# An attention and GEGLU block: the GEGLU part in a written order on every engine, gate logits on ScalarE, first loads in two slices, and every second turn of the attention with one block product more

## The chip, the core and the metric

The kernel runs on one core of a Trainium2 chip. The time is the device time of one execution in microseconds (us). A profile is one execution recorded by the hardware: it shows each engine's instructions (PE is TensorE's matmuls, PEld its weight loads, DVE VectorE, ACT ScalarE, POOL GpSimd, SP the queue of SyncE that issues most transfers). "L60" is line 60 of the kernel; all matmuls go through one helper at that line, so they are told apart by their tiles.

## What is computed

```
a = attention(x, w_qkv, w_o)            # 16 heads of 28, 2048 positions, width 448, no mask
g = x @ w_gate; u = x @ w_up            # 448 -> 1792
b = (gelu_tanh(g) * u) @ w_down         # 1792 -> 448
s = sigmoid(x @ gate_w)                 # one number per position
out = s * a + (1 - s) * b
```

All arrays are fp32, batch 1. The kernel keeps nearly fp32 precision by cutting an operand into a rounded part `hi` (format fp32r, a ScalarE copy) and the remainder `lo` (a subtraction on VectorE or GpSimd); a product of two such operands is hi x hi + hi x lo + lo x hi.

## The kernel before, in words

**Blocks of products.** A block is a result of 128 x 512. Its 448 long contraction is cut into 7 slices of 64 rows, so with the three products of the split a block has 21 matmuls (`UNITS`). A matmul uses 64 rows of the array, half of it; two blocks on the two row halves (g = 0, 1) advance side by side.

**Stage 1** loads and splits x and the weights, and makes Q and K (`pq`, 14 pairs of blocks), which are stored to DRAM, then V and the gate logits (`v_pair`, the logits copied by VectorE at L200). A bound on the scores is computed; VectorE, TensorE and ScalarE then pass a branch (`rows`, L295) around a slow path that this data does not need, with a hint put after the sixth `v_pair`. Loads go through raw buffers of one slice each (`AHEAD` of them).

**Stage 2, the attention.** For each head, key tile and half of the queries (a *turn*), `scores` makes a PSUM tile `sc` of 1024 columns by four matmuls of 64 rows, and ScalarE takes its exponential into `pt`. Since scores use one row half at a time, the other half takes up to four (`RATE`) products of the up and gate projections into the tile `pu` (one PSUM buffer): 68 (`NOUT`) of the 112 blocks of both projections are made here. A finished block is copied by VectorE to `u` (L429) and stored to DRAM (`ud`). After each four key tiles, at the third turn (`LATE`) of the next four, `values` adds these four tiles' `pt` times V into `po`. A *period* is these eight turns. After a head's last, `finish` copies `po` to `o` on VectorE, sends the sums through DRAM (`dend`, `r`), takes the reciprocal, sends it back in another layout (`rdend`, `rb`), multiplies, and stores the head to `od`. Two blocks run in an `sc` tile ahead of the first score (`two_blocks`), and what is left of the blocks at the end.

**Stage 3, the FFN.** The 14 tiles of the hidden dimension (f) go in seven chunks of two, in the order of `ORDER`. For each f and each half b the gate blocks `pg` that are still missing are made on TensorE, the others are loaded (`gs`); gelu (ACT), times `u` (DVE), split (ACT, DVE) give `hl2`. Then 16 tiles of `pd` (128 x 448, six matmuls each, four PSUM buffers) are added into `acc` on VectorE with the gate (`down`). For chunks 2 and 3 `project` puts attention output times WO in between (11 matmuls a tile); O is loaded through one raw buffer `oraw` and split on ACT, POOL and DVE (`load_o`, L591 to L603). The weights of an f come as `hraw` to `half` (one raw buffer, `load_half`) and as `draw` to `w` (`load_f`). In the last chunk the result goes to a tile named `gs` (two buffers) and is stored from there.

**What sets the order.** Instructions handed to `pin` (tc.keep_in_program_order) stay in the order of the program among themselves; the others are placed by a scheduler that works with its own costs. Before, all matmuls are pinned, and the loads and splits of stage 1; `finish`, the `u` copies and nearly all of stage 3 on DVE, ACT and SP are not. Each engine then executes its list in order and waits at an instruction whose inputs are not there.

## Time and profile before

| | |
|---|---|
| median of 3 runs | 1083.91 us (1083.66 to 1086.1) |
| the profiled execution | 1081.29 us, span of its trace 1079.5 us |
| granted TensorE clock, whole span | 0.99 |
| TensorE busy | 1047.9 us, 97% of the span |
| start to the last V product | 0 to 113.1 us |
| first products of the attention stage to the last `po` | 119.2 to 776.15 us |
| FFN, to TensorE's end | 776.15 to 1072.75 us |
| tail | 6.75 us |

A row of a timeline is: start, length, engine, line, operation, output <- inputs, count, and in brackets the idle time of the engine ahead of it with what ended it. A row of the chain of waits is: start, length, what was waited for or worked at.

### The profile page before, as it was taken

The numbers are of one execution on the slowest core, as the hardware profiler recorded it, in microseconds if no ns is written. First come the engines' busy times: TensorE is split into PE (matmuls) and PEld (weight loads), VectorE is DVE, ScalarE is ACT, GpSimd is POOL, SyncE is SP. The second block draws the span as 40 slices with busy tenths as digits, with TensorE's granted clock in tenths as the row PEclk, the third lists the DMA queues.
The fourth block names the chain that finished last, engine by engine and source line by source line (L and its number), as shares of the span: only waits on it lengthen the run. The fifth ranks groups of instructions, "written<-read, shape, count | busy, mean of one in ns | idle before, by whom it ended". The sixth has DMA issues, their size and how long they took to land.

```text
span 1079.5 us, 20134 instructions
## 1 busy us (share of the span) xinstructions
PE 1047.9 (97%) x8257; PEld 733.0 (68%) x8257; DVE 332.9 (31%) x515; ACT 612.3 (57%) x740; POOL 69.2 (6%) x47
## 2 busy tenths in 40 slices
PE   8999799999999999999999999999888999999997
PEld 6889555655665665565566556556576889888886
DVE  4552112111111111111111111111287656646644
ACT  5332377777777877777787777778344304131320
POOL 3524200000000000000000000000001011100000
PEclk9999899999999999999999999999998999999999
DMA  6795544345345344344354444422476314122313
GB/s 188 250 380 148 133 115 134 106 124 138 103 128 144 89 134 137 102 126 132 101 141 118 111 135 114 123 81 67 152 208 199 103 57 120 49 59 80 105 49 137
DMA packets 68321, 138.19 MB, mean 128 GB/s; under 512 B 15744, under 2 KB 25984, under 8 KB 62784
## 3 DMA queue, kind: packets, MB, share of 16 engines
q1 hardware_dynamic: 67904, 136.33, 42.8%
q8 instruction: 66, 1.08, 0.4%
q10 hardware_dynamic: 320, 0.52, 0.2%
q14 instruction: 31, 0.25, 0.1%
HBM read 96.44 MB, written 40.37 MB: 127 GB/s over the span
## 4 chain that ended last, share of the span: by engine, by line
PE 77%; DMA 4%; ACT 3%; DVE 3%; issue 2%; SPq 0%; DVEq 0%; ACTq 0%
PE po L60 21%; PE sc L60 21%; PE pu L60 16%; PE pd L60 11%; PE pg L60 8%; ACT pt L378 2%; DMA out<-gs 1%; DMA u<-ud 1%; DVE ohl L601 1%; DMA oraw<-in_wo 1%; DVE gs L578 1%; DMA oraw<-od 1%; DMA draw<-in_wd 1%; DVE g L554 0%; DMA gs<-ud 0%
## 5 line engine op out<-in xcount | busy, mean ns | idle before, releaser
L378 ACT ACTIVATE pt<-sc 128x1024 f32<-128x1024 f32 x512 | 477.7, 1041 | 170.6 <-PE sc L60 169.5
L60 PE MATMUL sc<-Q,K 64*128 64x512 f32 x2048 | 413.8, 399 | 0.6 <-ACT pt L378 0.4
L60 PEld LDWEIGHTS sc<-Q,K 64*128 64x128 f32 x2048 | 314.5, 184 | 83.3 <-issue 50.3
L60 PE MATMUL pu<-X,half 64*128 64x512 f32 x1344 | 317.4, 387 | 0.0
L60 PEld LDWEIGHTS pu<-X,half 64*128 64x128 f32 x1344 | 247.1, 184 | 33.9 <-issue 1.7
L60 PE MATMUL po<-pt,V 128*32 128x512 f32 x2048 | 234.4, 598 | 0.0
L60 PE MATMUL pd<-w,hl 128*128 128x448 f32 x672 | 145.5, 373 | 9.8 <-DVE acc L575 5.0
L60 PEld LDWEIGHTS po<-pt,V 128*32 128x32 f32 x2048 | 60.2, 110 | 139.5 <-issue 135.8
L429 DVE COPY u<-pu 128x512 f32<-128x512 f32 x64 | 43.8, 685 | 348.9 <-PE pu L60 289.4
L60 PEld LDWEIGHTS pd<-w,hl 128*128 128x128 f32 x672 | 126.4, 190 | 28.1 <-DVE acc L575 6.2
L60 PE MATMUL pg<-X,half 64*128 64x512 f32 x924 | 106.9, 388 | 0.0
L60 PEld LDWEIGHTS pg<-X,half 64*128 64x128 f32 x924 | 88.1, 184 | 18.5 <-issue 2.7
L60 PE MATMUL pq<-X,WQK 64*128 64x512 f32 x588 | 69.2, 394 | 3.1 <-ACT X L161 2.5
L60 PEld LDWEIGHTS pq<-X,WQK 64*128 64x128 f32 x588 | 56.1, 188 | 16.4 <-ACT X L161 3.3
L527 ACT ACTIVATE w<-draw 128x448 fp32r<-128x448 f32 x14 | 8.1, 578 | 92.8 <-PE pd L60 70.2
L575 DVE SCALAR_TENSOR_TENSOR acc<-pd,gate,acc 128x448 f32<-128x448 f32 x80 | 52.8, 681 | 17.0 <-PE pd L60 16.9
L599 POOL CAST ohl<-oraw 64x512 fp32r<-64x512 f32 x4 | 2.4, 606 | 800.2 <-DMA oraw<-od 698.9
L555 ACT ACTIVATE hl<-g 128x512 fp32r<-128x512 f32 x56 | 33.9, 629 | 24.8 <-DVE g L554 20.6
L554 DVE TENSOR_TENSOR g<-g,u 128x512 f32<-128x512 f32 x56 | 36.7, 687 | 33.3 <-ACT g L553 28.5
L556 DVE TENSOR_TENSOR hl<-g,hl 128x512 fp32r<-128x512 f32 x56 | 36.7, 689 | 9.2 <-ACT hl L555 8.3
L553 ACT ACTIVATE g<-pg 128x512 f32<-128x512 f32 x44 | 24.1, 593 | 26.3 <-PE pg L60 26.3
L60 PE MATMUL pd<-WO,ohl 128*128 128x448 f32 x176 | 36.7, 367 | 0.0
(65 smaller groups left out, 449.2 us busy)
## 6 DMA issues: line engine op xcount, KB each, us to landing
Q<-qkd SPq DMA_DIRECT2D x128, 224.0 KB
ud<-u SPq DMA_DIRECT2D x68, 256.0 KB
qkd<-hl SPq DMA_DIRECT2D x28, 512.0 KB
K<-qkd SPq DMA_DIRECT2D x64, 224.0 KB
u<-ud SPq DMA_DIRECT2D x56, 256.0 KB
rb<-rdend SPq DMA_DIRECT2D x64, 64.0 KB
hraw<-in_wu SPq DMA_DIRECT2D x28, 128.0 KB
od<-o SPq DMA_DIRECT2D x64, 56.0 KB
```

What stands on the lines that cost most here:

```text
L60: return pin(nc.tensor.matmul(o, lhsT, rhs, start=start, stop=stop))
L378: nc.scalar.activation(pt, sc, AF.Exp, scale=SCALE)
L429: nc.vector.tensor_copy(u, block["p"])
L527: nc.scalar.activation(hi, draw, AF.Copy)
L553: nc.scalar.activation(g, pg, AF.Gelu_apprx_tanh)
L554: nc.vector.tensor_tensor(g, g, u, OP.mult)
L555: nc.scalar.activation(hl[:, 0], g, AF.Copy)
L556: nc.vector.tensor_tensor(hl[:, 1], g, hl[:, 0].bitcast(F32), OP.subtract)
L575: nc.vector.scalar_tensor_tensor(acc[:, t], p, g1, acc[:, t], OP.mult, OP.add)
L578: nc.vector.scalar_tensor_tensor(y, p, g1, acc[:, t], OP.mult, OP.add)
L599: nc.gpsimd.tensor_copy(O[0:64, 3], o[0:64, 3])
L601: nc.vector.tensor_tensor(O[64:, 3], o[64:, 3], O[64:, 3].bitcast(F32), OP.subtract)
```

## The change

- **Stage 1.** Raw buffers hold two slices (5 of 1024 columns in place of 8 of 512); the first pieces go on two queues (SP and ACT's); a tiny ACT operation stands ahead of the first split; splits have another order, the later lo parts all on GpSimd. The gate logits are copied by ScalarE, and the branch hint is given for TensorE and ScalarE only.
- **Stage 2.** No blocks ahead of the first score. 66 blocks in place of 68 are made here (64 in `pu`, 2 with the `rest` at the end, in an `sc` tile, all in one `run`), so two gate blocks more are left for the FFN. In the turn ahead of `values` products are given only to finish a block, and if the number of products since the last `values` is odd, one product more is issued right ahead of `values`. `free` is aligned at `values`.
- **Stage 3.** Everything is pinned: loads, splits, gelu, accumulations and stores stand on every engine in the order of the program. The list `side_work` holds operations of which `step` issues one after the matmuls of each `down` or `project` tile, ahead of its accumulation: the rest of the gelu work, the four parts of the WO and O splits (now ScalarE and VectorE, no GpSimd), and `prepare` of the two f's of the next chunk. The result is written over `acc` and stored from there.

```diff
-NOUT = 68
+NOUT = 66
 ORDER = (0, 4, 1, 5, 2, 6, 3, 7, 8, 9, 10, 11, 12, 13)
-AHEAD = 8
-HL = 13
+AHEAD = 5
+HL = 12
 PAD = 112
-WARM = 9
+WARM = 12
...
-                d = pin(nc.vector.tensor_copy(gate[:, 0, i:i + 1], p[g][:, D:D + 1]))
-            return m, a, d
-
+                a = pin(nc.scalar.activation(gate[:, 0, i:i + 1], p[g][:, D:D + 1], AF.Copy))
+            return m, a
...
+        load(slice(0, 1))
+        for (c, srcs), a in ((pieces("x00")[0], 1), (pieces("w0")[1], 0)):
+            for g in range(2):
+                pin(nc.scalar.dma_start(out=raws[a][side(g), c], in_=srcs[g]))
+        issued = 2
+        while issued < AHEAD:
+            load()
+        pin(nc.scalar.activation(zero[:, 0:1], zero[:, 0:1], AF.Copy))
+        first = [parts(a, raws[i]) for i, a in enumerate(SPLITS[-1])]
+        for i, b in ((0, 0), (1, 0), (1, 1), (2, 0), (2, 1), (0, 1), (3, 0), (3, 1), (4, 0)):
+            r, hi, lo = first[i][b]
+            pin(nc.scalar.activation(hi, r, AF.Copy))
+            pin(nc.vector.tensor_tensor(lo, r, hi.bitcast(F32), OP.subtract))
+        done = len(first)
...
         def values(h, kt):
+            free[:] = [max(free)] * 2
             if kt == 0:
...
         def unit():
 
-            nonlocal hold
+            nonlocal hold, beside
             product(block)
+            beside += 1
             if block["n"] == len(UNITS):
+                put(block)
                 hold = 3
...
-        two_blocks()
...
-                    spaced(h, kt, half, 0 if due and count == LATE or count == LATE + 1 and h + kt > 3 else RATE)
-                    if due and count == LATE:
+
+                    turn = due and count == LATE
+                    if turn or count == LATE + 1 and (h or kt > 3):
+                        n = 0
+                    elif due and count == LATE - 1:
+                        n = 0 if block["n"] in (0, len(UNITS)) else RATE
+                    else:
+                        n = RATE + (h == 0 and kt <= ENDS[0] + 1)
+                    spaced(h, kt, half, n)
+                    if turn:
+
+                        hold = 0
+                        if beside % 2 and left():
+                            run([[unit], []] if block["g"] == 0 else [[], [unit]])
                         for a in due:
                             values(*a)
-                        due, hold = [], 0
+                        due, hold, beside = [], 0, 0
                 ready.append((h, kt))
                 if kt in ENDS:
                     ready, due, count = [], ready, 0
-        hold = 0
-        run([[], [unit] * left()] if block.get("g") else [[unit] * left(), []])
-        while NOUT - 1 - block["at"] >= 2:
-            two_blocks()
+
+        rest = [dict(block)]
+        sc = psc.tile([P, 1024], F32, name="sc")
+        for c in range(2):
+            start(sc[:, c * 512:(c + 1) * 512])
+            rest.append(dict(block))
+        todo = [[], []]
+        for b in rest:
+            todo[b["g"]] += [lambda b=b: product(b)] * (len(UNITS) - b["n"])
+        run(todo)
+        for b in rest:
+            put(b)
         for a in due:
             values(*a)
-        hold = 0
-        while left():
-            unit()
-            hold = 0
+        assert block["at"] == NOUT - 1
...
+        def load_w(f):
             draw = gp.tile([P, TB], F32, name="draw")[:, 0:D]
-            nc.sync.dma_start(out=draw, in_=wd[f * P:(f + 1) * P])
-            hi, lo = w[:, hi:hi + D], w[:, lo:lo + D]
-            nc.scalar.activation(hi, draw, AF.Copy)
-            nc.vector.tensor_tensor(lo, draw, hi.bitcast(F32), OP.subtract)
-            WD[f] = hi, lo
+            w = gp.tile([P, 2, TB], F32R, name="w", bufs=4)[:, :, 0:D]
+            pin(nc.sync.dma_start(out=draw, in_=wd[f * P:(f + 1) * P]))
+            pin(nc.scalar.activation(w[:, 0], draw, AF.Copy))
+            pin(nc.vector.tensor_tensor(w[:, 1], draw, w[:, 0].bitcast(F32), OP.subtract))
+            WD[f] = w
...
+        def tail(f, i, tb, pg):
+            u = tp.tile([P, TB], F32, name="u")
+            pin(nc.sync.dma_start(out=u, in_=ud[0, f, :, tb * TB:(tb + 1) * TB]))
+            if pg is None:
+                pg = tp.tile([P, TB], F32, name="gs", bufs=2)
+                pin(nc.sync.dma_start(out=pg, in_=ud[1, f, :, tb * TB:(tb + 1) * TB]))
+            g = tp.tile([P, TB], F32, name="g")
+            hl = HL2[i, tb]
+
+            def gelu():
+                pin(nc.scalar.activation(g, pg, AF.Gelu_apprx_tanh))
+                pin(nc.vector.tensor_tensor(g, g, u, OP.mult))
+
+            def parts():
+                pin(nc.scalar.activation(hl[:, 0], g, AF.Copy))
+                pin(nc.vector.tensor_tensor(hl[:, 1], g, hl[:, 0].bitcast(F32), OP.subtract))
+
+            return [gelu, parts]
+
+        def tails(f, i, tbs, pgs):
+            a, b = (tail(f, i, tb, pg) for tb, pg in zip(tbs, pgs))
+            return [a[0], b[0], a[1], b[1]]
...
+        def load_wo():
+            raw = wpo.tile([P, 4, TB], F32, name="oraw")[:, :, 0:D]
+            pin(nc.sync.dma_start(out=raw, in_=wo))
+            for b in range(4):
+                yield lambda b=b: (pin(nc.scalar.activation(WO[:, b], raw[:, b], AF.Copy)),
+                                   pin(nc.vector.tensor_tensor(WO[:, 4 + b], raw[:, b], WO[:, b].bitcast(F32), OP.subtract)))
+
...
+        def load_o(tb):
+            s = slice(tb * TB, (tb + 1) * TB)
+            o = wpo.tile([P, 4, TB], F32, name="oraw")
+            pin(nc.sync.dma_start(out=o[:, 0:3], in_=od[0:3 * P, s].rearrange("(b p) n -> p b n", p=P)))
+            pin(nc.sync.dma_start(out=o[:, 3], in_=od[3 * P:, s].unsqueeze(0).to_broadcast([2, 64, TB])))
+            O = OHL[tb] = wpo.tile([P, 7, TB], F32R, name="ohl")
+            for b in range(4):
+                r = slice(64, P) if b == 3 else slice(0, P)
+                lo = 3 if b == 3 else 4 + b
+                yield lambda b=b, r=r, lo=lo: (
+                    pin(nc.scalar.activation(O[:, b], o[:, b], AF.Copy)),
+                    pin(nc.vector.tensor_tensor(O[r, lo], o[r, b], O[r, b].bitcast(F32), OP.subtract)))
+
+        side_work = []
...
+        def step():
+            if side_work:
+                side_work.pop(0)()
+
+        def down(n, tb, chunk):
...
+                step()
                 g1 = gate[:, 2, t:t + 1]
...
+                    pin(nc.vector.scalar_tensor_tensor(acc[:, t], p, g1, acc[:, t], OP.mult, OP.add))
+                    pin(nc.sync.dma_start(out=out[0, t * P:(t + 1) * P], in_=acc[:, t]))
...
+        def prepare(f):
+            if here(f, 1):
+                load_half(1, f, by_act, pin)
+            load_w(f)
+
+        for f in chunks[0]:
+            prepare(f)
+        early = {}
+        for n, chunk in enumerate(chunks):
+            nxt = chunks[n + 1] if n + 1 < len(chunks) else ()
             for b in range(2):
                 for i, f in enumerate(chunk):
-                    if b == 0 and n * FC + i + 1 < NF:
-                        load_f(ORDER[n * FC + i + 1])
-                    for tb, hl in zip((b, b + 2), hidden(f, b)):
-                        hls.setdefault(tb, []).append(hl)
+                    if not here(f, b):
+                        if (n, b) not in early:
+                            for a in tails(f, i, (b, b + 2), (None, None)):
+                                a()
+                    else:
+                        side_work += gate_blocks(f, i, b)
+                        if (b, i) != (1, FC - 1):
+                            while side_work:
+                                step()
             if n == 1:
-                load_wo()
-            for i, tb in enumerate((0, 2, 1, 3)):
-                if n in (1, 2) and i % 2 == 1:
-                    load_o((n - 1) * 2 + i // 2)
-                down(n, tb, hls[tb])
-                if n in (2, 3) and i % 2 == 0:
-                    project((n - 2) * 2 + i // 2)
+                side_work += load_wo()
+            for k, tb in enumerate((0, 2, 1, 3)):
+                if (n, k) == (1, 1):
+                    side_work += load_o(0)
+                down(n, tb, chunk)
+                if n in (2, 3) and k in (0, 3):
+                    while side_work:
+                        step()
+                    at = (n - 2) * 2 + k // 3
+                    project(at)
+                    if at < NTB - 1:
+                        side_work += load_o(at + 1)
+                if nxt and k == 1:
+                    side_work += [lambda f=f: prepare(f) for f in nxt]
+                    for i, f in enumerate(nxt):
+                        if not here(f, 0):
+                            side_work += tails(f, i, (0, 2), (None, None))
+                            early[n + 1, 0] = 1
+            while side_work:
+                step()
```

How the written order reads on the engines, at three places. First TensorE around two successive `values` in the middle of the attention. Before, every period is alike (Q and K carry their buffer's number):

```order
L60 MATMUL pu<-X,half 128x512
L60 MATMUL sc<-Q_1441,K_1442 128x512 x8
L60 MATMUL po<-pt,V 32x512 x16
L60 MATMUL sc<-Q_1441,K_1442 128x512 x4
L60 MATMUL pu<-X,half 128x512
```

Now, the one with the product more:

```order
L60 MATMUL pu<-X,half 128x512
L60 MATMUL sc<-Q_1422,K_1423 128x512 x8
L60 MATMUL pu<-X,half 128x512
L60 MATMUL po<-pt,V 32x512 x16
L60 MATMUL sc<-Q_1422,K_1423 128x512 x5
L60 MATMUL pu<-X,half 128x512
```

A `pu` product of the next block stands between the eight score matmuls and `po`; in the period behind it the block needs one product less, and five score matmuls follow `po` alone.

Second, VectorE from the last head's `o` on, where the FFN begins. Before:

```order
L392 COPY o<-po 128x512
L556 TENSOR_TENSOR hl_10382<-g,hl_10382 128x512
L556 TENSOR_TENSOR hl_10388<-g,hl_10388 128x512
L528 TENSOR_TENSOR w<-draw,w 128x448 x2
L398 RECIPROCAL r<-r 128x16
L554 TENSOR_TENSOR g<-g,u 128x512 x3
```

Now:

```order
L403 COPY o<-po 128x512
L409 RECIPROCAL r<-r 128x16
L415 TENSOR_TENSOR o<-o,rb 128x512
L541 TENSOR_TENSOR w<-draw,w 128x448
L238 TENSOR_TENSOR half<-hraw,half 128x896
L541 TENSOR_TENSOR w<-draw,w 128x448
L558 TENSOR_TENSOR g<-g,u 128x512 x2
```

The reciprocal and the product with `rb` now stand ahead of the FFN's first splits; before, FFN work stood between and around them, and the first `half` ahead of `o`.

Third, VectorE in the downs of a late chunk (the L622 rows are the accumulations), now:

```order
L562 TENSOR_TENSOR hl_13_10293<-g,hl_13_10293 128x512
L622 SCALAR_TENSOR_TENSOR acc<-pd,gate,acc 128x448 x5
L238 TENSOR_TENSOR half<-hraw,half 128x896
L541 TENSOR_TENSOR w<-draw,w 128x448
L622 SCALAR_TENSOR_TENSOR acc<-pd,gate,acc 128x448
L238 TENSOR_TENSOR half<-hraw,half 128x896
L541 TENSOR_TENSOR w<-draw,w 128x448
L622 SCALAR_TENSOR_TENSOR acc<-pd,gate,acc 128x448 x7
```

The lo parts of both weights of both next f's stand around the accumulation of the ninth tile; before, the scheduler had spread them over the chunk.

183 lines of the change are left out of this document (58 added, 125 removed).

## The prediction

> **What bounds the kernel now.** I read the page's busy times and its chain first, then a table by stage, then the timelines of the places that the change touches.
>
> ```profile
> PE 1047.9 (97%) x8257; PEld 733.0 (68%) x8257; DVE 332.9 (31%) x515; ACT 612.3 (57%) x740; POOL 69.2 (6%) x47
> PE 77%; DMA 4%; ACT 3%; DVE 3%; issue 2%; SPq 0%; DVEq 0%; ACTq 0%
> ...
> 119.18:126.43 7.25, 6.41 (x42) 5.27 (x42) 0.69 (x1) 0.00 (x0) 0.00 (x0) 0.80 0.00 1
> 126.43:776.15 649.72, 646.22 (x5484) 388.79 (x5485) 98.12 (x149) 481.93 (x518) 0.00 (x0) 1.00 0.42 120
> 776.15:1072.75 296.60, 286.80 (x1776) 247.52 (x1772) 184.61 (x267) 87.89 (x142) 16.39 (x8) 0.99 0.34 105
> 1072.75:1079.50 6.75, 0.00 (x0) 0.00 (x0) 1.95 (x4) 0.00 (x0) 0.00 (x0) 0.88 0.37 136
> ```
>
> The columns of a stage are its length, then PE, weight loads, DVE, ACT and POOL, the granted clock, the DMA share and GB/s. TensorE is busy 97% of the span and carries 77% of the chain. So only three things can move the time: fewer or better paired matmuls, fewer gaps between them, and the ends where it has nothing. In the attention DVE is busy 98 of 650 us; in the FFN it is 185 of 297. There an engine that must work in a written order has the least slack.
>
> **The entry into the attention.** The rows are TensorE's, then VectorE's, then SyncE's.
>
> ```profile
> 109.66 3.42 PE L60 MATMUL pq<-WV,X 64*128 64x450 f32 x32
> 119.18 6.41 PE L60 MATMUL sc<-X,half 64*128 64x512 f32 x41 [6.11 <-DVEq L295]
> 126.43 0.49 PE L60 MATMUL sc<-X,half 64*128 64x512 f32 x1 [0.84 <-DVE u L429]
> 114.12 0.16 DVE L200 COPY gate<-pq 128x1 f32<-128x1 f32 x1 [0.28 <-ACT V L199]
> 111.10 1.43 SPq L345 DMA_DIRECT2D Q<-shd  x2
> ```
>
> TensorE ends the V products at 113.1 and stands 6.11 us until DVE's sequencer has passed the branch at L295: DVE still has gate logits to copy there, the last at 114.12. Then come the two blocks of `two_blocks` (6.4 us at a clock of 0.80), a stall of 0.84 on their copy, and the first score at about 126.4. Afterwards ScalarE copies the logits, DVE reaches the branch earlier, and both blocks are gone from here. The first score then needs only the Q rows, whose last load is issued by 112.5 and about 1 us later in the new order; with a landing some 2 us on (an estimate) it starts near 115.3: **-11.1**. It cannot start before 113.1 (-13.3); had DVE still to be waited for until 119.2, only 7.2 would go. The blocks' 42 products are not saved: they run in the FFN (below). A taken branch whose target is not in the two pages held stalls its engine for an instruction fetch, says the Trainium skill, "Runtime: NRT & Kernel Launch", section Instruction fetch mechanics; the 6.11 us agree. By it DVE, which loses its hint, still stalls, but before anyone needs it.
>
> The start of the program changes less. The first product stands 2.54 us for its X.
>
> ```profile
> 8.22 7.24 PE L60 MATMUL pq<-X,WQK 64*128 64x512 f32 x44 [2.54 <-ACT X L161]
> ```
>
> An earlier table load and the two parts on two queues can take away part of that, and larger pieces land later. I take **-0.8** (+1 to -1.5).
>
> **The periods of the attention.** A period is four key tiles; 64 run alike.
>
> ```profile
> 301.83 0.39 PE L60 MATMUL pu<-X,half 64*128 64x512 f32 x1
> 304.78 0.39 PE L60 MATMUL pu<-X,half 64*128 64x512 f32 x1
> 306.08 3.57 PE po L60 x32
> 314.72 0.39 PE L60 MATMUL pu<-X,half 64*128 64x512 f32 x1
> 314.73 1.29 PE L60 MATMUL sc<-Q,K 64*128 64x512 f32 x8
> 315.15 0.69 DVE L429 COPY u<-pu 128x512 f32<-128x512 f32 x1 [7.59 <-PE pu L60]
> 310.42 7.46 ACT L378 ACTIVATE pt<-sc 128x1024 f32<-128x1024 f32 x8 [2.47 <-PE sc L60]
> ```
>
> The last product before a copy comes every 9.94 us (304.78, 314.72). Within one, 13 products take from 301.83 to 304.78: the two row halves advance together every 0.227 us. A period has 32 score and 21 block products, 53: one half step stays empty. With 22 and 20 in turn nothing is empty, which at best saves one step of 0.227 in two periods, 32 x 0.227 = 7.3 us in all. But the extra product of the 22 belongs to a new block, block products have one PSUM buffer, and the copy that empties it starts at 315.15 and ends at 315.84. The free place beside the last score is four steps after 314.72, at 315.63. So that product, and the `po` products behind it, are 0.27 late at least, and I take 0.35 with the release and weight load. The period of 20 gains at most 0.227; its scores, however, follow the exps, which are spaced 0.93 (7.46 over 8) and with three score buffers hold the turn without products, so I take 0.1. Per two periods +0.25, over 31 of them **+7.8**. Ends: -7.3 if the copy is hidden, +11 if the shorter period gains nothing (0.35 x 31).
>
> **The end of the attention.**
>
> ```profile
> 762.84 4.57 PE L60 MATMUL sc<-X,half 64*128 64x512 f32 x37
> 770.29 0.94 PE L60 MATMUL sc<-X,half 64*128 64x512 f32 x2 [2.89 <-DVE u L429]
> 771.16 5.06 PE L60 MATMUL po<-pt,V 128*32 128x512 f32 x32
> 776.15 3.03 PE L60 MATMUL pg<-X,half 64*128 64x512 f32 x24
> ```
>
> A copy that DVE does late holds the rest blocks for 2.89 us, and this `po` group takes 5.06 where the others take 3.57. Filled in one run, with the FFN's work no longer mixed in ahead, both go: **-4.4** (-2 to -6).
>
> **The FFN.** Its work is priced by two long stretches, its present stalls by difference.
>
> ```profile
> 954.02 19.34 PE L60 MATMUL pg<-X,half 64*128 64x512 f32 x168
> 973.29 20.09 PE L60 MATMUL pd<-w,hl 128*128 128x448 f32 x96
> 993.31 0.97 PE L60 MATMUL pg<-X,half 64*128 64x512 f32 x6
> ```
>
> From 954.02 to 973.29 is 0.1147 per gate product, and the 20.02 to the next gate at 993.31 make 0.2085 for each of 96 of the down kind. Now 924 and 848 of them make 106.0 + 176.8 = 282.8 of 296.6: stalls of 13.8. Two gate blocks more are 42 x 0.1147 = **+4.8**. Then, in the written order, three stalls stand new.
>
> First, its start. DVE's order runs: copy of the last head, reciprocal, product with `rb`, lo of `w`, lo of the first `half`. The first gate group needs that lo at its second pair. Here is the same chain in the middle of the attention:
>
> ```profile
> 369.49 0.69 DVE L392 COPY o<-po 128x512 f32<-128x512 f32 x1 [3.84 <-PE po L60]
> 375.51 0.25 DVE L398 RECIPROCAL r<-r 128x16 f32<-128x16 f32 x1 [5.33 <-DMA r<-dend]
> 380.59 0.69 DVE L404 TENSOR_TENSOR o<-o,rb 128x512 f32<-128x512 f32 x1 [4.28 <-DMA rb<-rdend]
> 778.98 0.62 DVE L528 TENSOR_TENSOR w<-draw,w 128x448 fp32r<-128x448 f32 x1 [0.73 <-ACT w L527]
> 790.85 0.68 DVE L404 TENSOR_TENSOR o<-o,rb 128x512 f32<-128x512 f32 x1
> 970.16 1.09 DVE L228 TENSOR_TENSOR half<-hraw,half 128x896 fp32r<-128x896 f32 x1
> ```
>
> 11.1 us pass from the copy to the end of the DMA waits (two round trips), then 0.69 + 0.62 + 1.09: TensorE stands **13.5** (12 if less DMA traffic shortens the trips, 17 by the last head of before, whose product began at 790.85, 14.6 after the end of its `po` at 776.2). Before, the first gate half was split ahead of the chain, and gate products began at 776.15 at once.
>
> Second, chunk 1 to 2. One raw buffer serves WO and O, and SyncE holds the next `hraw` behind it; the O splits now lie in DVE's order between the accumulations.
>
> ```profile
> 808.75 5.70 DMA oraw<-od
> 815.13 4.07 DVE L601 TENSOR_TENSOR ohl<-oraw,ohl 64x512 fp32r<-64x512 f32 x1 [2.78 <-ACT ohl L600]
> ```
>
> With D the start of the downs (1.25 us a tile): the last WO split ends at D+9.5, O lands near D+16 (5.7 after the release), four splits and accumulations (0.69 + 0.68 each) end at D+21.8, the first half follows at 22.9 and frees `hraw`, which lands again 4.4 later (below), and with 0.95 + 1.09 the half of f=6, the first that the next gates need, is there at D+29 instead of D+20: **+9** (5 to 10). An operation of 512 columns on VectorE takes 0.69 elsewhere (380.59), not 4.07: the long one stood beside POOL's. In the Trainium skill, "SBUF — State Buffer", section SBUF: two separate sides, the port pair that VectorE and GpSimd share is an exclusive lock, so a GpSimd operation blocks the other for its whole length; 4.07 beside 0.69 agrees. By it the change would win 3.4 us per O load, but on an engine that here waits for the load.
>
> Third, chunks 2 to 6. `prepare` of both f's stands in steps 8 and 9 of the downs, and `hraw` has one buffer.
>
> ```profile
> 971.28 0.47 SPq L84 DMA_DIRECT2D hraw<-in_wg  x1
> 975.67 0.95 ACT L327 ACTIVATE half<-hraw 128x896 fp32r<-128x896 f32 x1 [1.13 <-DMA hraw<-in_wg]
> 980.72 0.47 SPq L84 DMA_DIRECT2D hraw<-in_wg  x1
> 983.50 0.68 DVE L575 SCALAR_TENSOR_TENSOR acc<-pd,gate,acc 128x448 f32<-128x448 f32 x1 [0.48 <-PE pd L60]
> ```
>
> From the release (971.2) to the landing (975.67) it takes 4.4. The first half's lo ends at D+11.5; the second lands at D+15.9, ACT takes 0.95, its lo and `w` end at D+18.7. Accumulation 9 waits behind them and ends at 19.4, and the fourteenth tile, which needs its PSUM buffer (there are four), wanted to start at 16.25: 3.2 late, some 3.4 with queues, four times: **+13.6** (8 to 16). Before, the scheduler put the two loads 9.4 us apart (971.28, 980.72).
>
> So the stalls are 13.5 + 9 + 13.6 = 36.1 in place of 13.8: FFN +4.8 + 22.3 = **+27.1**.
>
> **The tail.**
>
> ```profile
> 1072.12 1.30 DVE L578 SCALAR_TENSOR_TENSOR gs<-pd,gate,acc 128x448 f32<-128x448 f32 x2 [1.48 <-DMA out<-gs]
> 1074.94 1.28 DVE L578 SCALAR_TENSOR_TENSOR gs<-pd,gate,acc 128x448 f32<-128x448 f32 x2 [1.52 <-DMA out<-gs]
> ```
>
> Two `gs` buffers pace the last results in pairs, 2.8 us apart; TensorE ends 6.75 before the span. Stored from `acc` nothing waits: one result, one store, some 4.2 in all: **-2.5** (-1.5 to -3.3).
>
> **Sum**: -0.8 - 11.1 + 7.8 - 4.4 + 27.1 - 2.5 = +16.1. The profiled execution took 1081.3 us (span 1079.5), so 1097.4; the median of the runs shown lies 2.6 above it: **1100 us**, about 1.5% slower.
>
> **The rivals.** (1) *DVE's waits in the chunks are hidden*: loads land early enough, or the four PSUM buffers cover them, and only the start of the FFN stalls. Then 9 + 13.6 go: 1077.4, faster. For it: of 20 us of downs DVE works about 17 (16 accumulations of 0.68, two halves, two `w`, four tail operations of 0.69). Against it: the one `hraw` buffer fixes the order release, load, split. It decides the sign once chunk stalls are under 6.5 us together. Chance 0.13. (2) *The pairing does what it is made for*: the copy comes in time, the attention gains 7.3 instead of losing 7.8: 1085, no change. Against it stands 315.84 against 315.63. Chance 0.09. (3) *The start costs 17, O and `hraw` loads share the queue with stores and take 2 us more each*: +3.5 + 8, 1111. Chance 0.10. (4) *The entry still waits for DVE's branch*, now without a hint, until 119.2: 7.2 gained instead of 11.1, 1104, slower too; 0.05.
>
> **How the numbers follow.** The likeliest, 1100, has 0.63, its own range is 1092 to 1107. The range down to 1083 takes in (2), up to 1111 takes in (3) and (4). Within 0.3% (1080.7 to 1087.2, about what the runs can tell from no change) lies (2): 0.09; faster is (1): 0.13; slower the rest, 0.78.
>
> **What would show it.** The changed kernel's timeline: the first score near 115; `pu` ahead of each second `po` released by `DVE u`, and a pair of periods of 20.1 us or more instead of 19.88; after the last `po` a gap of 12 us or more ending at `DVE half`; in the downs waits for `DVE acc` late in each chunk, with DVE waiting for `ACT half` or the load of `hraw`. I am wrong if the FFN, from the last `po` to TensorE's end, is under 305 us, or if the pair of periods falls under 19.9.

## The result

The changed kernel takes 1127.99 us (1126.53 to 1129.53, 4 runs) where the kernel before takes 1083.79 (1082.9 to 1086.1, 4 runs): 1.0405 times as long, 95% interval 1.0383 to 1.0426. I had forecast 1100. The direction was right, the size was not: 44 us were lost in place of 16.

The page of the changed kernel shows the span, the busy time of each engine (with its share of the span and its number of instructions) and the shares of the chain of waits:

```profile
span 1126.1 us, 20095 instructions
PE 1066.5 (95%) x8260; PEld 744.0 (66%) x8260; DVE 326.6 (29%) x513; ACT 615.5 (55%) x769; POOL 52.1 (5%) x39
PE 81%; DMA 8%; DVE 4%; ACT 2%; SPq 2%; issue 2%; POOL 1%; POOLq 0%; DVEq 0%; ACTq 0%
```

TensorE has almost the same number of matmuls, is busy 19 us longer with them, and the span is 47 us longer. VectorE is busy less than before. So nothing became too much work for an engine: TensorE waits more, and some of its work is slower. The table by stage of the changed kernel (columns as in the prediction: length, PE, weight loads, DVE, ACT, POOL, granted clock, DMA share, GB/s) says where:

```profile
0.00:115.12 115.12, 109.84 (x965) 90.96 (x965) 45.35 (x80) 42.05 (x93) 50.05 (x39) 1.00 0.76 233
115.12:122.99 7.87, 0.22 (x1) 0.03 (x1) 0.00 (x0) 1.11 (x4) 2.02 (x1) 0.80 0.93 188
122.99:775.97 652.98, 652.37 (x5481) 392.21 (x5481) 94.01 (x144) 477.12 (x513) 0.00 (x0) 1.00 0.40 113
775.97:789.47 13.50, 0.80 (x4) 0.29 (x4) 3.17 (x5) 1.52 (x2) 0.00 (x0) 0.60 0.28 81
789.47:825.40 35.93, 33.04 (x178) 27.69 (x179) 22.97 (x37) 15.45 (x25) 0.00 (x0) 0.91 0.59 171
825.40:871.53 46.13, 32.68 (x184) 28.14 (x184) 24.92 (x41) 14.39 (x25) 0.00 (x0) 0.88 0.45 133
871.53:1122.25 250.72, 237.53 (x1452) 204.64 (x1452) 135.51 (x207) 63.83 (x108) 0.00 (x0) 0.95 0.29 87
1122.25:1126.10 3.85, 0.00 (x0) 0.00 (x0) 0.68 (x1) 0.00 (x0) 0.00 (x0) 1.00 0.32 119
```

The FFN shows a granted clock of 0.60 to 0.95 where it was 0.99 before. Set beside the kernel before and my terms (stage lengths from the two profiled executions, in us):

| stretch | before | changed | difference | my term |
|---|---|---|---|---|
| start to the end of the V products | 113.1 | 115.1 | +2.0 | -0.8 |
| from there to the first score | 13.7 | 7.9 | -5.8 | -11.1 |
| first score to the end of the last `po` | 649.4 | 653.0 | +3.6 | +7.8 - 4.4 |
| FFN, to TensorE's end | 296.6 | 346.3 | +49.7 | +27.1 |
| tail | 6.8 | 3.9 | -2.9 | -2.5 |

The FFN again, as time over the price of its matmuls (0.1147 us for each of `pg`, 0.2085 of `pd`), from the starts of the stretches in the timelines:

| part of the FFN | before | changed | my term |
|---|---|---|---|
| start and gates of chunk 0 | 0.1 | 16.3 | 13.5 |
| downs of chunk 0 | 5.1 | 3.5 | 0 |
| chunk 1, and the wait for the gates of chunk 2 | 7.6 | 17.5 | 9 |
| downs of chunks 2 to 5 | 0 | 4.5 + 5.9 + 6.0 + 4.9 = 21.3 | 13.6 |
| the rest | 1.0 | 0.1 | 0 |

Here is TensorE at the start of the FFN and in the downs of chunk 4:

```profile
784.35 0.80 PE L60 MATMUL pg<-X,half 64*128 64x512 f32 x2 [8.37 <-ACT half L337]
789.47 12.48 PE L60 MATMUL pg<-X,half 64*128 64x512 f32 x82 [4.33 <-DVE half L238]
...
1012.67 16.38 PE L60 MATMUL pd<-w,hl 128*128 128x448 f32 x78
1032.24 6.54 PE L60 MATMUL pd<-w,hl 128*128 128x448 f32 x18 [3.19 <-DVE acc L622]
1038.70 19.34 PE L60 MATMUL pg<-X,half 64*128 64x512 f32 x168
```

The stand (a wait in which TensorE is idle) of 3.19 us for accumulation 9 is the one I had worked out (3.2). But the 18 products behind it then take 6.5 us, and at 0.2085 each they should take 3.8. At the start, 82 gate products take 12.4 in place of 9.4. The granted clock, the share of its full speed that TensorE is given, tells why:

```profile
1028.80:1032.24 3.44, 0.25 (x3) 0.85 0.71 238
1032.24:1037.00 4.76, 4.76 (x13) 0.50 0.02 9
1037.00:1038.70 1.70, 1.70 (x7) 0.70 0.00 0
```

(length, PE, clock, DMA share, GB/s). After the stand the clock is 0.50 for nearly 5 us.

### The profile page after: what moved, and what is told of

Same layout as the page of the kernel before. It is cut to its first block, busy times and chain, and to the rows that moved or that the text cites. A ratio compares the mean times of both kernels' runs of the same rounds, so it can differ in the third digit from the quotient of the medians.

```text
span 1126.1 us, 20095 instructions
## 1 busy us (share of the span) xinstructions
PE 1066.5 (95%) x8260; PEld 744.0 (66%) x8260; DVE 326.6 (29%) x513; ACT 615.5 (55%) x769; POOL 52.1 (5%) x39
## 4 chain that ended last, share of the span: by engine, by line
PE 81%; DMA 8%; DVE 4%; ACT 2%; SPq 2%; issue 2%; POOL 1%; POOLq 0%; DVEq 0%; ACTq 0%
PE sc L60 33%; PE po L60 20%; PE pd L60 10%; PE pg L60 9%; PE pq L60 5%; PE pu L60 4%; DMA hraw<-in_wg 1%; DMA raw<-in_xT 1%; DMA oraw<-od 1%; DMA gs<-ud 1%; DVE half L238 1%; DMA hraw<-in_wu 1%; DVE acc L622 1%; DMA draw<-in_wd 1%; ACT pt L388 1%
## 5 line engine op out<-in xcount | busy, mean ns | idle before, releaser
L60 PEld LDWEIGHTS sc<-Q,K 64*128 64x128 f32 x2048 | 308.3, 185 | 118.4 <-issue 60.8
L60 PE MATMUL pu<-X,half 64*128 64x512 f32 x1344 | 327.7, 391 | 0.0
L60 PE MATMUL pd<-w,hl 128*128 128x448 f32 x672 | 152.1, 387 | 21.0 <-DVE acc L622 18.1
L60 PEld LDWEIGHTS pd<-w,hl 128*128 128x128 f32 x672 | 132.8, 200 | 39.9 <-DVE acc L622 20.4
L60 PE MATMUL pg<-X,half 64*128 64x512 f32 x966 | 116.9, 400 | 21.2 <-ACT half L337 16.5
L60 PEld LDWEIGHTS pg<-X,half 64*128 64x128 f32 x966 | 94.9, 191 | 43.0 <-ACT half L337 17.8
L622 DVE SCALAR_TENSOR_TENSOR acc<-pd,gate,acc 128x448 f32<-128x448 f32 x80 | 53.3, 680 | 16.3 <-PE pd L60 16.1
L561 ACT ACTIVATE hl<-g 128x512 fp32r<-128x512 f32 x56 | 34.8, 632 | 17.5 <-DVE g L558 17.5
L238 DVE TENSOR_TENSOR half<-hraw,half 128x896 fp32r<-128x896 f32 x29 | 31.6, 1090 | 25.2 <-ACT half L337 24.6
L337 ACT ACTIVATE half<-hraw 128x896 fp32r<-128x896 f32 x12 | 11.4, 946 | 49.4 <-DMA hraw<-in_wg 49.4
L599 ACT ACTIVATE ohl<-oraw 128x512 fp32r<-128x512 f32 x16 | 8.9, 620 | 51.2 <-PE pd L60 37.7
```

Source lines behind the costliest of these rows:

```text
L60: return pin(nc.tensor.matmul(o, lhsT, rhs, start=start, stop=stop))
L238: mark(nc.vector.tensor_tensor(w[:, NS:], raw, w[:, 0:NS].bitcast(F32), OP.subtract))
L337: return nc.scalar.activation(o, i, AF.Copy)
L561: pin(nc.scalar.activation(hl[:, 0], g, AF.Copy))
L599: pin(nc.scalar.activation(O[:, b], o[:, b], AF.Copy)),
L622: pin(nc.vector.scalar_tensor_tensor(acc[:, t], p, g1, acc[:, t], OP.mult, OP.add))
```

## The experiments

Each is named by its label, and times are medians. The changed kernel's 1128.0 was measured beside 1083.8 for the kernel before; beside the experiments that kernel took 1084.0 to 1085.9. A difference of about 2 us from 1128.0 is therefore not clear of the drift.

### Which stage carries the loss: e3_ffn_before

```diff
-        def load_w(f):
...
-        def step():
...
-        def prepare(f):
...
+        def load_f(f):
...
+        def hidden(f, b):
...
+        load_f(ORDER[0])
...
```

> The changed kernel with the third stage (FFN) as it was before the change, placed by the scheduler; stages 1 and 2 are the changed ones. Theory: the third stage carries the loss: it takes about 301 us (296.6 and two gate blocks) in place of 346, the tail 6.8 again in place of 3.9; 1083 to 1089 us, more if the scheduler mixes FFN work into the end of the attention again (+4). Rival: what was lost follows from the late last head and the first two stages: over 1100 us.

Measured: 1093.6 us (1092.2 to 1094.3), ratio to the kernel before 1.0069 (1.0051 to 1.0087). 34 of the 44 us go; the FFN takes 307.7 in place of 346.3. It was to be 301: the downs of chunk 0 stand 13.5 over their price here, 5.1 in the kernel before. The scheduler, which places this FFN, meets another end of the attention; that this is the reason was not tested. The third stage carries most of the loss; the first two stages with this FFN still leave about 8 us.

### The one raw buffer and the order of prepare: e1c_spread

```diff
+                    if nxt and k == 0:
+                        side_work.append(lambda f=nxt[0]: prepare(f))
                     if at < NTB - 1:
                         side_work += load_o(at + 1)
+                elif nxt and k == 0:
+                    side_work.append(lambda f=nxt[0]: prepare(f))
                 if nxt and k == 1:
-                    side_work += [lambda f=f: prepare(f) for f in nxt]
+                    side_work.append(lambda f=nxt[1]: prepare(f))
```

> The changed kernel (1128 us) with the first f of the next chunk prepared from the fifth tile of the downs on and the second from the ninth, in place of both in the ninth and tenth; a second raw buffer does not fit in the memory. Theory: what chunks 2 to 5 lose comes from the one hraw buffer, whose second load starts only at the first half's split, one step before it is needed; it makes the stand of TensorE and, through the clock, the slow products behind it. With four steps (5 us) between the two, the load of 4.3 us is hidden: the 21.3 us of these chunks go, and some of chunk 1 to 2: 1103 to 1108 us. Rival 1, only the stands go and the slow products stay: 1113 to 1116. Rival 2, VectorE's written order is too full anyway: 1124 to 1130.

Measured: 1109.4 us (1107.9 to 1111.4), 18.6 less. That is just short of what I expected, since chunk 1 gained nothing. The downs of chunk 5, where the changed kernel stood 3.1 us:

```profile
1044.35 20.09 PE L60 MATMUL pd<-w,hl 128*128 128x448 f32 x96
1064.37 5.97 PE L60 MATMUL pg<-X,half 64*128 64x512 f32 x50
```

No stand and no slow product is left in chunks 2 to 5: they are 0.4 under their price together, 21.7 us better. Chunk 1 got 1.1 worse in all (18.6 over): the half of f=2 now stands ahead of the O splits, and its last piece waits for the O transfer of which the next experiment but one tells. So the order release, load, split through one buffer is the cause, and VectorE's written order as such is not too full. The four accumulation tiles between the two prepares are all the cure. The other cure, a second `hraw` buffer, has no room: with it 30.5 KB of a partition are left where the next pool needs 32.

### What a stand costs beyond itself: e8_filled

```diff
                 p = psd.tile([P, D], F32, name="pd")
+                if n in (2, 3, 4, 5) and (tb, i) == (3, 1):
+                    fills = [psg.tile([P, TB], F32, name="pg") for _ in range(2)]
+                    for _ in range(14):
+                        for g in range(2):
+                            mm(fills[g], X[side(g), 0, 0:P], X[side(g), 0, 0:TB], True, True)
```

> The changed kernel with 14 pairs of matmuls that nobody needs (3.2 us at full clock) ahead of the fourteenth tile of the downs of chunks 2 to 5, where TensorE otherwise stands 3.1 to 3.5 us for the accumulation. They take nothing away of the wait itself. Theory: the stand makes the granted clock fall to 0.50 for some 4 to 6 us after it, which costs 1.5 to 2.8 us each time; with TensorE busy the clock stays at 1.00, the products after the wait run at 0.2085 us each at once, and the time falls by 7 to 9 us to 1119 to 1121. Rival, the products after a stand are slow for another reason (the weights, the buffers): no change or longer, 1126 to 1132.

Measured: 1123.8 us (1122.7 to 1125.8), 4.2 less, though TensorE does 112 matmuls more. The same place in chunk 4:

```profile
1013.79 16.38 PE L60 MATMUL pd<-w,hl 128*128 128x448 f32 x78
1030.10 3.47 PE L60 MATMUL pg<-X 64*128 64x512 f32 x28
1033.77 3.92 PE L60 MATMUL pd<-w,hl 128*128 128x448 f32 x18 [0.20 <-DVE acc L627]
```

and its clock (length, PE, clock, DMA share, GB/s):

```profile
1030.10:1033.77 3.67, 3.48 (x30) 1.00 0.78 252
1033.77:1037.61 3.84, 3.84 (x18) 1.00 0.00 1
```

The wait is no shorter (3.67 us from the end of the products ahead, 3.3 in the changed kernel). It is filled with products that nobody reads, and the clock stays at 1.00; the 18 products behind take 3.84 us in place of 6.46. In the changed kernel the slow products behind the four stands cost 1.4, 2.5, 2.7 and 1.7 us over their price, 8.3 together, and the stands 13.2; with fill only the waits are left, each a little longer than there, and the downs stand 15.1 over the price of the wanted products in place of 21.3. These 6 us are a little less than the 7 to 9 that I expected. The execution shown, the longest of the four, gave 4 of them back ahead of that: its last `po` is 1.3 later, and chunks 0 and 1 take 2.7 more.

### The O transfer: e2_o_two_loads

```diff
-            pin(nc.sync.dma_start(out=o[:, 3], in_=od[3 * P:, s].unsqueeze(0).to_broadcast([2, 64, TB])))
+            for a in (0, 64):
+                pin(nc.sync.dma_start(out=o[a:a + 64, 3], in_=od[3 * P:, s]))
```

> The changed kernel with the last quarter of O loaded by two transfers of 64 rows, as before the change, in place of one transfer with a leading broadcast of 2. Theory: the one transfer takes 11 us to land (847.5 to 858.6; the two of before landed together in 5.7), VectorE and a piece of the next hraw wait for it, and chunk 1 to 2 loses 16.1 us instead of my 9. With two transfers it loses some 9: 1119 to 1122 us, and less in the later O loads. Rival: it lands as late, since the rings are full then: 1126 to 1130 us.

Measured: 1125.8 us (1123.9 to 1127.6), 2.2 less, nearer to the rival and hardly clear of the drift; what follows rests on the profiled executions. In the changed kernel the transfer, the piece of `hraw` behind it and VectorE read so (the row of the chain of waits):

```profile
847.48 11.14 DMA oraw<-od
```

and, in the timeline, SyncE and VectorE:

```profile
851.80 0.68 SPq L84 DMA_DIRECT2D hraw<-in_wg  x1
858.63 0.47 SPq L85 DMA_DIRECT2D hraw<-in_wg  x1
859.30 0.69 DVE L600 TENSOR_TENSOR ohl<-oraw,ohl 64x512 fp32r<-64x512 f32 x1 [3.38 <-ACT ohl L599]
863.93 1.09 DVE L238 TENSOR_TENSOR half<-hraw,half 128x896 fp32r<-128x896 f32 x1 [3.22 <-ACT half L337]
```

and with two transfers, VectorE:

```profile
855.10 0.69 DVE L601 TENSOR_TENSOR ohl<-oraw,ohl 128x512 fp32r<-128x512 f32 x1 [5.19 <-ACT ohl L600]
858.81 0.69 DVE L601 TENSOR_TENSOR ohl<-oraw,ohl 64x512 fp32r<-64x512 f32 x1
862.47 1.09 DVE L238 TENSOR_TENSOR half<-hraw,half 128x896 fp32r<-128x896 f32 x1 [2.26 <-ACT half L337]
```

The last split no longer waits, and chunk 1 with the wait behind it falls from 17.5 to 14.0 over its price: the transfer was worth 3.5 us there, not 7, as the first O parts now land later (VectorE stands 5.19 for them). The profiled execution is 4.0 us shorter, the median 2.2; the other stands of the FFN differ by 1 to 3 us from one execution to the next. In the Trainium skill, "DMA: Bandwidth & Descriptors", section Rules for kernel authors, a leading broadcast of c copies confines a transfer to at most c of the 16 DMA engines. The 11.1 us of this one with c = 2, against 5.7 for the two transfers of before, agree in direction; which engines carried it no row shows. I had read over its line in the diff.

### The product more at the turns: e4_no_extra

```diff
-                        if beside % 2 and left():
-                            run([[unit], []] if block["g"] == 0 else [[], [unit]])
```

> The changed kernel without the product more at every second turn. Theory: that product waits for the copy of the finished block, two periods take 20.14 us in place of 19.88, and 31 such pairs cost 8 us: 1118 to 1121 us, pairs of 19.8 to 19.9. Rival (what the even count is made for): without it a half step stays empty in each period, and the time is the same or up to 7 us longer.

Measured: 1122.7 us (1119.6 to 1123.9), 5.3 less. From the chain of waits, three successive `po` groups of the changed kernel:

```profile
305.58 3.57 PE po L60 x32
315.91 3.57 PE po L60 x32
325.73 3.57 PE po L60 x32
```

and of this one:

```profile
303.47 3.57 PE po L60 x32
313.39 3.57 PE po L60 x32
323.31 3.57 PE po L60 x32
```

Here two periods take 20.15 with the product more (10.33 and 9.82) and 19.84 without; over the whole stage the means are 20.13 and 19.88. From the first score to the last `po` it is 645.9 in place of 653.0, 7.1 us; that the median falls by 5.3 is within what the FFN varies (348.5 here).

### The entry: e5_two_blocks and b1_gate_act

In the changed kernel, blocks ahead of the first score again:

```diff
-NOUT = 66
+NOUT = 68
...
         load_head(0)
+        two_blocks()
```

> The changed kernel with the two blocks ahead of the first score again (68 blocks in the attention, two less in the FFN). Theory for the entry: not VectorE's branch but the loads of Q and K (12 transfers of 224 KB at some 0.2 MB per us, 13 us) set the first score at 123.0, so the two blocks run in a wait of 7.9 us that is there anyway: the first score stays at 123 to 124 and the FFN is shorter by 4.8: 1122 to 1124 us. Rival, my prediction's step: the blocks stand in the way, the first score comes 6 to 7 us later, 1128 to 1131 us.

Measured: 1117.7 us (1112.5 to 1118.1), 10.3 less. TensorE there:

```profile
116.53 5.05 PE L60 MATMUL sc<-X,half 64*128 64x512 f32 x42 [1.19 <-ACT gate L198]
122.49 0.47 PE L60 MATMUL sc<-Q,K 64*128 64x512 f32 x1 [0.68 <-DMA Q<-shd]
```

The first score comes at 122.5, as in the changed kernel without blocks (123.0): the blocks run in a wait that is there anyway, and what they wait for in the end is the last load for Q. The FFN is 8.7 shorter, 4.8 of them for two blocks and 3.8 at the turn to chunk 2, which now needs one gate half (f=6) in place of two; this turn I had not counted when I expected 1122 to 1124. Some 2 us more come at the entry: the first score is 0.5 earlier, and the products behind it run at a clock of 1.00 (122.50 to 126.00), in the changed kernel at 0.50 (122.99 to 126.60).

In the kernel before, the gate logits alone:

```diff
-                d = pin(nc.vector.tensor_copy(gate[:, 0, i:i + 1], p[g][:, D:D + 1]))
-            return m, a, d
+                a = pin(nc.scalar.activation(gate[:, 0, i:i + 1], p[g][:, D:D + 1], AF.Copy))
+            return m, a
```

> The kernel before with one part of the change alone: gate logits copied by ScalarE, branch hint on TensorE and ScalarE only. Theory: there TensorE stands 6.1 us for VectorE's branch, with two blocks (6.4 us) behind it; the loads of Q and K, which end near 117.5 us (the DMA share falls from 0.91 to 0.23 at 116 to 120), are hidden by both. With the wait gone the blocks run from 113 on and the first score comes near 120.5 in place of 126.8: 5 to 6 us less, 1078 to 1080 us where the kernel before takes 1084. So this part gains when the blocks stay, and it was their removal that left its gain to the loads. Rival: VectorE without its hint is waited for all the same: no change, 1083 to 1086 us.

Measured: 1076.4 us (1074.8 to 1079.3), ratio 0.993 (0.9912 to 0.9948).

```profile
114.31 5.06 PE L60 MATMUL sc<-X,half 64*128 64x512 f32 x41 [1.19 <-ACT gate L200]
120.31 0.50 PE L60 MATMUL sc<-X,half 64*128 64x512 f32 x1 [0.94 <-DVE u L429]
120.85 0.46 PE L60 MATMUL sc<-Q,K 64*128 64x512 f32 x1
```

The stand of 6.11 for VectorE's branch is 1.19 now, and the first score comes at 120.9 in place of 126.8. This part of the change gains 6 to 8 us, if the two blocks stay.

### The first gate half of the FFN: e7_early_half

```diff
         run(todo)
+        load_half(1, ORDER[1], by_act, pin)
         for b in rest:
...
-            if here(f, 1):
+            if here(f, 1) and (1, f) not in halves:
```

> The changed kernel with the first gate half of the FFN (f=4) loaded and split ahead of the last head's copy, as before the change. My prediction's step: the 13.3 us at the start of the FFN stand for that half, and go with it; 1113 to 1117 us. Rival, from the trace: the first downs wait for the gelu of f=0, whose loads SyncE issues only after the last head's stores (789.6 to 791.4 us, landed at 795.5), so the stand only moves from before the gate products to behind them, and no more than 1 to 3 us go: 1125 to 1128 us.

Measured: 1123.5 us (1122.2 to 1125.5), 4.5 less.

```profile
776.52 9.81 PE L60 MATMUL pg<-X,half 64*128 64x512 f32 x84
798.31 1.84 PE L60 MATMUL pd<-w,hl 128*128 128x448 f32 x3 [11.97 <-ACT hl L562]
```

The gate products run at once and at full pace, and then TensorE stands 11.97 us for `hl`. The stand moved from ahead of the gates to behind them. The first downs come at 798.3 in place of 801.9.

### The tail: b2_out_acc

```diff
-                    y = tp.tile([P, TB], F32, name="gs", bufs=2)[:, 0:D]
-                    nc.vector.scalar_tensor_tensor(y, p, g1, acc[:, t], OP.mult, OP.add)
-                    nc.sync.dma_start(out=out[0, t * P:(t + 1) * P], in_=y)
+                    nc.vector.scalar_tensor_tensor(acc[:, t], p, g1, acc[:, t], OP.mult, OP.add)
+                    nc.sync.dma_start(out=out[0, t * P:(t + 1) * P], in_=acc[:, t])
```

> The kernel before with the result written over acc and stored from it. Theory: the pairs of 2.8 us at the end go, the tail is 3.9 us in place of 6.8: 1080.5 to 1082 us. Rival: the scheduler, which places this stage, orders something else for it; within 1 us of the kernel before.

Measured: 1081.3 us (1077.9 to 1083.0), ratio 0.9972 (0.996 to 0.9984), 2.7 less. The last results no longer come in pairs 2.8 apart but one by one at TensorE's pace:

```profile
1072.99 0.68 DVE L577 SCALAR_TENSOR_TENSOR acc<-pd,gate,acc 128x448 f32<-128x448 f32 x1 [0.56 <-PE pd L60]
1074.23 0.68 DVE L577 SCALAR_TENSOR_TENSOR acc<-pd,gate,acc 128x448 f32<-128x448 f32 x1 [0.55 <-PE pd L60]
```

### Do the causes add up: c1_all

The changed kernel with the edits of e5, e4, e1c, e2 and e7 together.

> The changed kernel with five mends together: the two blocks ahead of the first score again (68 blocks), no product more at the turns, the two prepares five tiles apart, O's last quarter by two transfers, the first gate half of the FFN split early. Theory: the causes are separate stands, so the single gains (10, 5 to 7, 18.6, 2 to 3.5, 4.5 us) add up, 40 to 43 of the 44: 1084 to 1090 us, with chunk 0 and the start of the FFN, which no mend touches fully, still some 15 over their price. Rival: the stands take each other's place, as that of the first gate half did: 1095 us and more.

Measured: 1085.5 us (1080.9 to 1087.8), ratio 1.0008 (0.9996 to 1.002). The single gains are 10.3 + 5.3 + 18.6 + 2.2 + 4.5 = 40.9 us; together they are 42.5. They add up within the drift. What is left over the price in its FFN is 12.7 at the first downs, 5.4 in chunk 0's and 12.5 in chunk 1's; every later chunk is at its price.

### What beats both: b3_both and b4_stage2

b3 is the kernel before with the edits of b1 and b2.

> The kernel before with both: gate logits on ScalarE, and the result stored from acc. If the two gains stand at two ends and don't touch, they add up: 8 to 9 us less, 1075 to 1077 us; it would be faster than both kernels. Rival: part of the one is lost in the other: 1079 to 1082.

Measured: 1073.05 us (1070.7 to 1074.5), ratio 0.99 (0.9884 to 0.9916), 11 us less than the kernel before. The two gains (7.6 and 2.7) stand at two ends and add up.

b4 is b3 with the attention stage of the changed kernel, blocks ahead and no product more.

> The kernel before with gate logits on ScalarE and the result stored from acc (1073.05 us), and the attention stage of the changed kernel, with the two blocks at its start and without the product more. Theory: of the changed attention stage only that product loses; the rest, a product order aligned at the turns and one run at the end, gains 3 us from first score to last product with V (644.9 us in the kernel with five mends, 648.1 in the one with two): 1069 to 1071 us, faster than both kernels. Rival: the scheduler, which places the FFN of before beside another end of the attention, gives it back in the first two chunks' downs (they took 20 us more than their price with the changed attention, 13 with the old): 1074 to 1079 us.

Measured: 1074.1 us (1073.4 to 1075.1), ratio 0.9902 (0.9882 to 0.9922): no different from b3. Its attention is 3.7 us shorter (644.4 in place of 648.1), and the downs of chunks 0 and 1 take it back (17.5 over their price, in b3 12.0): the rival. What those two chunks wait for was not taken apart in the kernels that the scheduler places.

## Why the prediction was right or wrong

**What failed most is the FFN's +27.1, which measured +49.7:** 22.6 of the 30.5 us that the profiled execution took beyond my sum. The step behind it: I added up TensorE's waits and put the products behind a wait at their full pace. They ran at a granted clock near 0.50, some 11 us in the FFN; a mis-sized load of O and the downs of chunk 0, put at nothing, make most of the rest. The entry failed by another step.

**The entry (-11.1, measured -5.8): the step that failed here is "a landing some 2 us on".** I took the last small load of Q for what the first score waits for, and a short landing for it. It stands behind twelve loads of 224 KB, eight of them issued from 108.62 on. SyncE and TensorE in the changed kernel:

```profile
108.62 3.95 SPq L292 DMA_DIRECT2D Q<-qkd  x8
115.89 3.88 SPq L298 DMA_DIRECT2D K<-qkd  x4
122.99 0.76 PE L60 MATMUL sc<-Q,K 64*128 64x512 f32 x1 [7.65 <-DMA K<-qkd]
```

In the stage table the stand from 115.12 to 122.99 has a DMA share of 0.93 at 188 GB/s. At that rate the twelve, 2.7 MB, take some 14 us (an estimate), whoever waits. The loads of K at 115.89 are the next head's. In e5 they are issued only at 123.49 and the first score comes at 122.5 all the same, so they delay it by little, if at all. That the loads and not VectorE's branch are the bound is shown from both sides: the blocks put back do not delay the first score (e5), and taking VectorE out of the way while the blocks stay gains 6 us (b1). I had priced the two blocks as time won at the entry and paid in the FFN; they had been hiding the loads. And the stand has a second price: the products behind it run at a clock of 0.50 until 126.6, some 1.7 us that the stage table counts in its next row. The bound I gave for this term (7.2 gained at worst) was also too kind, as it saw only VectorE.

**The start (-0.8, measured +2.0)** went the other way, beyond the end I gave (+1). The trace shows one place: GpSimd splits two slices of X ahead of the weights of the third tile, and the products wait for these.

```profile
18.95 2.54 POOL L160 TENSOR_TENSOR X<-raw,X 128x512 fp32r<-128x512 f32 x2 [1.91 <-ACT X L159]
22.78 9.59 PE L60 MATMUL pq<-X,WQK 64*128 64x512 f32 x82 [1.34 <-POOL WQK L160]
```

By 25 us the changed kernel is 2 us behind and stays there. No experiment changed this order, so that it is the cause is read from the trace and not shown by a run.

**The periods (+7.8) and the end of the attention (-4.4): right, and the close agreement of their sum is luck.** Two periods take 20.15 where I had 20.13, the product more waits for the copy as worked out, and taking it away gains 7.1 us in that stage (e4). The rival that the pairing does what it is made for falls. (The copy ends 0.21 behind the free place, 315.84 less 315.63, not 0.27; as I took 0.35, nothing follows from it.) The two terms together were +3.4, and the stage is +3.6. But by the starts of the `po` groups the periods cost +6.1 and the end -5.0; the other +2.5 lie between the first score and the first `po`, which I had at nothing, 1.7 of them the slow clock of the entry. And I read one row of the end wrongly: the `po` group of 5.06 us stood behind a wait of 2.89 and ran at clocks of 0.57 (770.29 to 773.00) and 0.83 (to 776.15). Its length was the clock and not the FFN's work mixed in.

**The start of the FFN (13.5, measured 13.3 of standing): right in size, incomplete in cause.** The product with `rb` begins 11.1 us after the copy of `o` (776.07 to 787.18), to the tenth what the middle of the attention showed, and the half comes behind it. But with the half ready TensorE stands nearly as long a little later (e7), since SyncE issues the loads for the first gelu only behind the last head's stores (the order in its trace; no run varied it). I named one thing that was late and not the next one. And the gates behind the stand ran at half clock, 3.0 us that I had not.

**Chunk 1 to 2 (9, measured 17.5 in chunk 1 and the wait behind it).** My chain of steps was right, O, its splits, then the two halves one after the other. Its first size was wrong: "O lands near D+16 (5.7 after the release)" took the duration of a row for two transfers of 64 rows for a transfer written in another way. It took 11.1, with a piece of `hraw` behind it, and 3.5 of the missing 8.5 go with it (e2). Between 3 and 4 are products at the slow clock behind the stands of 3.27 and 8.16 us there; the rest was not taken apart.

**Chunks 2 to 5 (13.6, measured 21.3): the mechanism was right, the term was mis-sized.** The waits for accumulation 9 are 3.5, 3.3, 3.2 and 3.1 us, where I had 3.2 and took 3.4. Spreading the two prepares takes all of it away (e1c). The missing 7.7 are the half clock behind each wait (8.3 in all); filling the wait keeps the clock (e8). In the kernel before no stand of this kind lies in these chunks, and its FFN shows 0.99. But its chunk 1 has one of 4.46 us, with clocks of 0.50 and 0.60 behind it (831.11 to 836.00), and two rows that I quoted show the same: the `po` group above, and the entry, 7.25 us at 0.80 behind a stand of 6.11. I read past both. The Trainium skill, "TensorE: Matmul & The Clock Gate", section HAM oscillation — how this bites in real kernels, says that TensorE must have no idle gaps over some 3.4 us. The rows agree in kind, but the measured limit is lower and not sharp: stands of 3.1 to 3.5 were enough here, and shorter ones in other kernels (the last section). By that rule the stand of 13.5 us that I forecast for the start of the FFN already had a second price, and the rule spoke against this change; I left it out.

**The tail (-2.5, measured -2.9): right** (b2: 2.7 by itself).

**The rivals.** None of them came. The third, for a slower kernel, had the loads longer and put them at 1111; neither it nor the forecast had the clock or the loads of the entry. Of the 30.5 us that the profiled execution took beyond my sum, some 11 are the slow clock behind stands in the FFN (3.0 at its start, 8 in chunks 2 to 5), 8.5 chunk 1, where the clock again has a part, 5.3 the entry, 2.8 the start, and 3.5 the downs of chunk 0, which I had at nothing although they were 5.1 over their price before.

## What to carry to other kernels

Price a long stand of TensorE twice: its length, and the products behind it at a lower clock. Here the four stands of 3.1 to 3.5 us cost 1.4 to 2.7 us more each. If a wait can't be moved, even useless products in it can pay, as in e8. Where work is written out in order, one buffer between load and split makes the distance between two uses of it the thing to choose: here four steps in between cost nothing, and one step cost 5 us each time. Before taking work away from ahead of a wait, add up the bytes that are in flight there: here two blocks that seemed to delay the entry were its cover.

## What was not expected of the hardware

Behind a stand of 3.2 us the granted clock was 0.50, and it stayed there for 4.8 us of continuous products (1032.24 to 1037.00). At the start of the FFN, where TensorE had two products in 13 us, it came back only after some 6 us of work (the changed kernel's clock by stretches, columns as above):

```profile
792.00:795.00 3.00, 3.00 (x16) 0.50 0.86 277
795.00:798.00 3.00, 3.00 (x26) 0.89 0.33 126
```

So 112 matmuls that nobody needs made a kernel 4 us faster.

The length of a stand alone does not say whether the clock falls. In e3, 12 products behind a stand of 2.38 us should take 2.5 us:

```profile
817.51 4.10 PE L60 MATMUL pd<-w,hl 128*128 128x448 f32 x12 [2.38 <-DVE acc L592]
```

Their clock is 0.73 and then 0.50. In b3 a stand of 2.19 us (803.42) is followed by 0.60 and one of 2.91 (764.45) by 1.00, and in e2 one of 3.30 (1075.64) is followed by 1.00. What decides between them was not found.
